# 32 unused bytes among the constants, which move the address of every tile allocated after them

## The chip, the cores and the metric

The kernel runs on one core of one Trainium2 chip. Its time is device microseconds of one execution. Three runs of the kernel before took 2201.70, 2201.96 and 2203.12 us; the median is 2201.96 us.

## What is computed

The reference runs sink-and-window attention on 4 batches of 8 heads, 768 tokens and head size 64, and feeds the result, as 3072 tokens of 512 features, to 8 experts whose weights come from a Sinkhorn iteration:

```
scores = scale * q @ k.T, kept where key < 4 or 0 <= query - key < 128
a = exp(scores - max) / (sum + 1e-9);   x = (a @ v) as 3072 x 512
P = exp(x @ w_gate - max); 8 times: P /= row sums; P /= column sums; P *= N / E
for e in range(8): out += P[:, e:e+1] * (max(x @ w1[e], 0) @ w2[e])     # 512 -> 1024 -> 512
```

## The kernel before

The whole of it is float32, and accuracy is kept by splitting an operand into a rounded half (type fp32r) and the rest; a product then has three matmuls (half by half, half by rest, rest by half).

**Attention, 0 to about 347 us.** Units of 128 queries and four heads; TensorE makes transposes (L428, L488, L504), scores (L467) and values (L524), and fills its gaps with the first expert's plain products for the first 1024 tokens (L598, with 256 columns, and L614, with 512).

**Part 0, about 347 to 942 us.** Experts 1 to 7 on the same 1024 tokens. An expert's hidden layer is cut into units of 256 columns, 28 in all. The first product of a unit (`first`, `product`, L725) is made as seven products of half size, named M1 to M7, on sums and differences of blocks: each is six matmuls of 128x128 by 128x512. The second product (`second`, L993) takes eight tiles of 128 tokens, each six matmuls with h, the hidden block, as the stationary operand and W2f, the weights, as the moving one. `STEPS` (L1030) lays them out: 15 steps of six matmuls, or 90 in a unit. The second product belongs to the unit before. h has one buffer in either of two pools, which take turns: `hps` (L1128) is `hp0` for even units and `hpr` for odd ones. Meanwhile the split weights are written to device memory for later (w1s, w2s), and SyncE's queue carries that traffic.

**Parts 1 and 2, about 942 to 2190 us.** All 8 experts on tokens 1024 to 3071, 1024 a part, 32 units a part. The first product is L725 again, 42 matmuls a unit, with W1q (reloaded split weights) stationary and the blocks B11, B21, B22 or T1 to T4 of x moving. The second product (`second2`, L1296) is seven products of half size as well, 42 matmuls a unit, with W2q stationary and hf, the split hidden layer, moving. `STEPS2` lays out one step of L725 and then one or two of L1296: three steps of L725 (M2, M1, M5) follow each other at a unit's start. A list by hand (`tick`, `at`) sets the order of all this; no scheduler moves it.

A matmul in the program is a pair of instructions: LDWEIGHTS reads the stationary operand, 128 columns, and MATMUL streams the moving one past it. The profile lists them as PEld and PE.

**Where tiles lie.** Each tile pool is a stretch of a partition's bytes. Pools that name no side are stacked from the bottom up, in the order in which they are opened: `const`, `xpool`, `accp`, and then the pools of each stage. Pools with `side="right"` are stacked from the top down: `hpr`, `w2pr`, `b12` (L360), `wa` and `rawp` of the attention stage, and later `w2q` and `accq` (L1395). In `const` the tiles of the Sinkhorn iteration are made after Xt.

Of the kernel before, what the change touches and what calls it, by code (L numbers as in the profile page):

```python
# [9 lines left out]
F32 = mybir.dt.float32  # L10
# [6 lines left out]
P = 128  # L17
# [212 lines left out]
def tile_sink_attention_moe(ctx: ExitStack, tc: tile.TileContext, q, k, v, wg, w1, w2, out):  # L230
# [27 lines left out]
    const = ctx.enter_context(tc.tile_pool(name="const", bufs=1))  # L258
# [56 lines left out]
        nc.vector.tensor_add(sel, ident[0:2 * E, 0:E], ident[0:2 * E, E:2 * E])  # L315

    Xt = const.tile([P, NT + 1, E + 1], F32, name="Xt")
    Pt = Xt[:, 0:NT, 0:E]

    xscr = dram.tile([KC, P, N], F32, name="xscr")  # L320
# [1128 lines left out]
```

## Time and profile before

| | us |
|---|---|
| median of three runs | 2201.96 |
| the profiled execution | 2202.73 |
| its span on the core | 2200.9 |
| TensorE busy (PE) | 2170.2, 99% of the span |
| TensorE weight loads (PEld), beside PE | 1774.1, 81% |
| VectorE (DVE) | 1561.5, 71% |
| ScalarE (ACT) | 893.1, 41% |
| GpSimd (POOL) | 742.5, 34% |
| DMA, share of 16 engines' time | 65.9% |

A busy PE is not PE at its peak: matmuls are pipelined, so what tells their price is how far their starts, or whole pieces of a chain, lie apart. The median is 0.77 us under the profiled execution.

### The profile page before, as it was taken

To read this page: it belongs to the slowest core of one execution; us is meant where nothing else is said; L and a number is where in the kernel's file an instruction comes from. 1 tells how busy PE (TensorE), PEld (TensorE's weight loads), DVE (VectorE), ACT (ScalarE), POOL (GpSimd) and SP (SyncE) were. 2 spreads that over 40 slices of the span, in tenths; PEclk is the share of its full clock that TensorE was granted. 3 is DMA by queue.
4 is the path that set the end of the run, shared out by engine and by line. 5 is a ranking of instruction groups with operands and counts; after the bars stand their busy time and mean duration, and the time that the engine had idled before them with its cause. 6 is when DMAs were issued, how large, how long until landed. Compare 5 with 4: busy or idle time off the path is not lost.

```text
span 2200.9 us, 31963 instructions
## 1 busy us (share of the span) xinstructions
PE 2170.2 (99%) x10525; PEld 1774.1 (81%) x10525; DVE 1561.5 (71%) x2888; ACT 893.1 (41%) x1914; POOL 742.5 (34%) x963
## 2 busy tenths in 40 slices
PE   7999999999999999999999999999999999999998
PEld 5888887788888888788888888888788888888886
DVE  8878868777777776776666666666756666666666
ACT  6777753544444443433323332322333233323222
POOL 6655544233233232133222233222332222332322
PEclk9999999999999999999999999999999999999999
DMA  6333324989898987776666666667866666666662
GB/s 169 87 81 89 81 88 151 313 285 308 280 313 278 315 275 240 247 268 202 191 198 200 197 190 200 203 191 244 301 198 198 201 200 192 199 202 188 201 192 82
DMA packets 395819, 453.31 MB, mean 206 GB/s; under 512 B 99648, under 2 KB 263680, under 8 KB 394752
## 3 DMA queue, kind: packets, MB, share of 16 engines
q1 hardware_dynamic: 395648, 451.20, 65.9%
q8 instruction: 86, 1.41, 0.3%
q14 instruction: 85, 0.70, 0.1%
HBM read 313.64 MB, written 137.46 MB: 205 GB/s over the span
## 4 chain that ended last, share of the span: by engine, by line
PE 92%; DVE 4%; ACT 2%; issue 1%; POOL 1%; DMA 0%; SPq 0%; DVEq 0%; ACTq 0%; POOLq 0%
PE c L725 39%; PE o L1296 20%; PE held L1296 8%; PE o L993 7%; PE held L993 7%; PE O L524 3%; PE ps L467 2%; PE g L598 2%; PE pt L488 2%; PE o L614 1%; PE pt L428 1%; ACT sc L473 1%; DVE T L752 0%; PE O L554 0%; DVE PT L351 0%
## 5 line engine op out<-in xcount | busy, mean ns | idle before, releaser
L751 ACT CAST hf<-w 128x512 fp32r<-128x512 f32 x448 | 265.7, 621 | 564.8 <-POOL w L1263 301.6
L1296 PE MATMUL o<-hf,W2q 128*128 128x512 f32 x1920 | 483.5, 395 | 0.0
L1296 PEld LDWEIGHTS o<-hf,W2q 128*128 128x128 f32 x1920 | 360.2, 188 | 85.7 <-DVE acc L1307 0.5
L725 PE MATMUL c<-T,W1q 128*128 128x512 f32 x1530 | 391.5, 391 | 0.0
L752 DVE TENSOR_TENSOR hf<-w,hf 128x512 fp32r<-128x512 f32 x448 | 330.4, 766 | 61.4 <-ACT hf L751 54.7
L1307 DVE TENSOR_TENSOR acc<-o,acc 128x512 f32<-128x512 f32 x300 | 206.6, 689 | 187.0 <-PE o L1296 186.8
L725 PEld LDWEIGHTS c<-T,W1q 128*128 128x128 f32 x1530 | 287.0, 188 | 63.3 <-ACT M L1240 0.4
L725 PE MATMUL c<-B,W1q 128*128 128x512 f32 x1134 | 279.3, 390 | 0.0
L1263 POOL TENSOR_TENSOR w<-w 128x512 f32<-128x512 f32 x64 | 83.2, 1300 | 513.2 <-DVE w L1245 508.0
L725 PEld LDWEIGHTS c<-B,W1q 128*128 128x128 f32 x1134 | 212.7, 188 | 46.2
L1244 DVE TENSOR_TENSOR w<-c,M 128x512 f32<-128x512 f32 x192 | 132.7, 691 | 153.1 <-PE c L725 148.3
L1240 ACT COPY M<-c 128x512 f32<-128x512 f32 x192 | 112.8, 588 | 264.8 <-PE c L725 264.0
L1296 PE MATMUL held<-hf,W2q 128*128 128x512 f32 x768 | 199.1, 395 | 0.0
L725 PE MATMUL c<-T,W1f 128*128 128x512 f32 x672 | 174.2, 394 | 2.0 <-DVE C L964 1.7
L993 PE MATMUL held<-W2f,h 128*128 128x512 f32 x672 | 173.7, 393 | 0.0
L993 PE MATMUL o<-W2f,h 128*128 128x512 f32 x672 | 173.7, 394 | 0.0
L1296 PEld LDWEIGHTS held<-hf,W2q 128*128 128x128 f32 x768 | 144.0, 188 | 33.5
L1278 POOL TENSOR_TENSOR w<-w 128x512 f32<-128x512 f32 x64 | 105.7, 1652 | 177.7 <-DVE hf L752 177.7
L814 POOL TENSOR_TENSOR r<-r 128x256 f32<-128x256 f32 x28 | 20.7, 740 | 397.1 <-ACT M L956 236.1
L725 PEld LDWEIGHTS c<-T,W1f 128*128 128x128 f32 x672 | 125.7, 188 | 32.4 <-issue 2.4
L993 PEld LDWEIGHTS o<-W2f,h 128*128 128x128 f32 x672 | 126.1, 188 | 29.6 <-DVE acc L1000 0.3
L993 PEld LDWEIGHTS held<-W2f,h 128*128 128x128 f32 x672 | 125.9, 188 | 29.0
(205 smaller groups left out, 3143.4 us busy)
## 6 DMA issues: line engine op xcount, KB each, us to landing
W2q<-w2s SPq DMA_DIRECT2D x448, 256.0 KB
W1q<-w1s SPq DMA_DIRECT2D x444, 256.0 KB
w1s<-W1f SPq DMA_DIRECT2D x56, 896.0 KB
w2s<-WT SPq DMA_DIRECT2D x136, 256.0 KB
r<-in_moe_w_dram SPq DMA_DIRECT2D x64, 512.0 KB
w2s<-W2f SPq DMA_DIRECT2D x56, 256.0 KB
PB<-psd SPq DMA_DIRECT2D x16, 512.0 KB
w2s<-W2f SPq DMA_DIRECT2D x56, 128.0 KB
```

What stands on the lines that cost most here:

```text
L467: nc.tensor.matmul(ps[h], lhsT=Q[r0:r0 + D, a, pr, :], rhs=K[r0:r0 + D, c, pr, :], start=(j == 0), stop=(j == 2))
L524: nc.tensor.matmul(u["O"][:, pr], lhsT=x_, rhs=y_, start=(j == 0), stop=(j == len(ops) - 1))
L725: nc.tensor.matmul(ps, lhsT=w1(a, k), rhs=x[:, b, k, :], start=(start and j == 0), stop=(stop and j == len(TERMS) - 1), skip_group_check=n ...
L751: nc.scalar.copy(dst[:, 0], src)
L752: at(1, lambda: nc.vector.tensor_sub(dst[:, 1], src, f32(dst[:, 0])))
L993: nc.tensor.matmul(o, lhsT=h[c, th][:, a, off:off + P], rhs=W2F[n][:, w, c, :], start=(begin and c == 0 and j == 0), stop=(end and c == 1 ...
L1240: nc.scalar.copy(t, T["c2"])
L1244: nc.vector.tensor_add(w, T["c1"], T[m])
L1263: nc.gpsimd.tensor_sub(S3, T["A11"], T["A21"])
L1278: at(k, lambda: nc.gpsimd.tensor_sub(T["A11"], w, T["A11"]))
L1296: nc.tensor.matmul(o, lhsT=W2Q[part, n, m][:, a, k * P:(k + 1) * P], rhs=F[part, n, H_OF[m]][:, w, :], start=(j == 0 and (begin or not hol ...
L1307: nc.vector.tensor_add(sums[m, k], o, sums[m, k])
```

## The change

```diff
     Xt = const.tile([P, NT + 1, E + 1], F32, name="Xt")
+
+    const.tile([P, 8], F32, name="pad")
     Pt = Xt[:, 0:NT, 0:E]
```

The new tile is 32 bytes in each partition. Nothing reads or writes it. All five engines have the same instructions in the same order as before, on the same tiles; no row of their order differs but for line numbers, which are two higher behind the new lines.

What differs are addresses. Everything that the left stack allocates after Xt lies 32 bytes higher; the right stack, ident, ones and Xt stay. In bytes within a partition, modulo 512 (all tiles of a row agree, since their sizes and the offsets within them are multiples of 512):

| tiles | used as | before | after |
|---|---|---|---|
| B11, B21, B22, T1 to T4 (left) | moving in L725 | 448 | 480 |
| W1f (left, part 0), W1q (left, parts 1 and 2) | stationary in L725 | 448 | 480 |
| h of pool hp0 (left; units 0, 2, ...) | stationary in L993 | 448 | 480 |
| h of pool hpr (right; units 1, 3, ...) | stationary in L993 | 480 | 480 |
| W2f (right) | moving in L993, L614 | 480 | 480 |
| hf (left) | moving in L1296 | 448 | 480 |
| W2q (right) | stationary in L1296 | 480 | 480 |
| W1 (right), B12 (right) | stationary, and one of four moving blocks, in L598 | 480 | 480 |
| PT and V (left) | both operands in L524 | 288 | 320 |
| ident (left, ahead of the new tile) | moving in the transposes | 288 | 288 |
| accumulators, copies, sums, raw weights of the experts (left) | other engines, DMA | 448 | 480 |

448 is a multiple of 64, and 480 is 32 more than one.

## Rows read from the trace of the kernel before

**Rows 1.** The page: the chain of waits, share of the span by engine and line.
```profile
PE 92%; DVE 4%; ACT 2%; issue 1%; POOL 1%; DMA 0%; SPq 0%; DVEq 0%; ACTq 0%; POOLq 0%
PE c L725 39%; PE o L1296 20%; PE held L1296 8%; PE o L993 7%; PE held L993 7%; PE O L524 3%; PE ps L467 2%; PE g L598 2%; PE pt L488 2%; PE o L614 1%; PE pt L428 1%; ACT sc L473 1%; DVE T L752 0%; PE O L554 0%; DVE PT L351 0%
```

**Rows 2.** Busy time by stretch: start:end, length, then by engine; clock, DMA share.
```profile
0.00:347.00 347.00, 329.15 (x2529) 279.76 (x2530) 275.14 (x976) 237.30 (x746) 207.44 (x495) 1.00 0.39 97
390.00:930.00 540.00, 539.46 (x2335) 437.51 (x2334) 400.13 (x606) 241.89 (x449) 155.26 (x191) 1.00 0.87 287
970.00:1570.00 600.00, 600.00 (x2605) 488.79 (x2604) 396.71 (x579) 182.63 (x316) 174.97 (x127) 1.00 0.69 215
1595.00:2170.00 575.00, 575.00 (x2497) 468.40 (x2497) 379.25 (x556) 177.65 (x307) 165.14 (x119) 1.00 0.64 193
```

**Rows 3.** Waits of PE, 390 to 2180 us: total us, times, longest.
```profile
PE c L725 <- DVE h L960: 1.8, 1, 1.8
...
PE c L725 <- ACT M L956: 0.2, 1, 0.2
```

**Rows 4.** The page: the granted clock in 40 slices of the span.
```profile
PEclk9999999999999999999999999999999999999999
```

**Rows 5.** Chain of waits, part 1, one unit: start us, us, what.
```profile
1312.59 4.09 PE c L725 x18
1316.68 1.39 PE held L1296 x6
1318.08 1.37 PE c L725 x6
1319.45 1.40 PE o L1296 x6
1320.84 1.37 PE c L725 x6
1322.22 2.79 PE o L1296 x12
...
1331.94 4.09 PE c L725 x18
```

**Rows 6.** Chain of waits, part 0, second product from hpr, then from hp0.
```profile
557.10 4.12 PE c L725 x18
561.22 1.38 PE o L993 x6
...
566.74 1.38 PE o L993 x6
568.13 1.37 PE held L993 x6
569.50 1.39 PE c L725 x6
...
577.79 4.11 PE c L725 x18
581.90 1.40 PE o L993 x6
...
587.47 1.40 PE o L993 x6
588.87 1.40 PE held L993 x6
...
598.66 4.12 PE c L725 x18
```

**Rows 7.** Chain of waits in attention, around three pieces of L598.
```profile
208.97 0.90 PE g L598 x6
...
211.25 0.70 PE o L614 x3
...
215.16 0.91 PE g L598 x6
...
221.76 0.90 PE g L598 x6
```

**Rows 8.** Line 960 on DVE in those units: durations ns min/median/max.
```profile
L960 DVE SCALAR_TENSOR_TENSOR h<-C,h x3: 691/693/693, 561.4 to 572.3; 128x512 fp32r<-128x512 f32 x3
L960 DVE SCALAR_TENSOR_TENSOR h<-C,h x3: 692/692/1225, 582.0 to 594.3; 128x512 fp32r<-128x512 f32 x3
```

**Rows 9.** Busy time in these two units of part 0, as in Rows 2.
```profile
557.10:577.79 20.69, 20.69 (x91) 16.89 (x91) 13.81 (x22) 9.04 (x17) 4.31 (x6) 1.00 0.97 309
577.79:598.66 20.87, 20.87 (x91) 16.90 (x91) 15.01 (x22) 9.31 (x17) 8.00 (x10) 1.00 0.76 241
```

## The prediction

> **What bounds the kernel now.** I read the chain of waits first: 92% of it is TensorE, and the lines L725, L1296 and L993 alone hold 39, 28 and 14% [rows 1]. The table of stretches then says where that is strict: from 390 to 930 us PE is busy 539.46 of 540 us, from 970 to 1570 and from 1595 to 2170 us all the time, while DVE, the next engine, has 400, 397 and 379 us of work there [rows 2]. The list of waits agrees: from 390 to 2180 us its longest entry is a single wait of 1.8 us [rows 3]. The clock is granted in full in every slice [rows 4], 1.00 in these stretches [rows 2], which is the level of 2.4 GHz. So in some 1750 us of the span the time is the number of matmuls times the distance of their starts, and nothing else. A change that moves no instruction can act there only through that distance.
>
> The distance is not one number. In part 1 a piece of six matmuls of L725 takes 1.37 us, a piece of six of L1296 1.39 to 1.40, though both stream 512 columns against 128x128 weights [rows 5]. Eighteen of L725 in a row take 4.09 us. The twelve by which that piece is longer than a piece of six took 4.09 - 1.37 = 2.72 us: 226.7 ns each, with no border in them. That is the price of a matmul whose neighbours are of its own kind: L725, both operands at 448. L1296 has moving hf at 448 and stationary W2q at 480, and pays 1.40 / 6 = 233 ns, 6.6 ns more.
>
> Two kinds of work could differ for another reason than addresses, so I looked for one line whose operand changes place. In part 0 the second product L993 streams W2f, at 480, in all units; h lies at 480 in one unit (pool hpr) and at 448 in the next (hp0). The pieces take 1.38 and, where a second one follows directly, 1.37 us in the first case, and 1.40 us each in the second [rows 6]. Length, shape, weights and order of the steps are the same. The units last 577.79 - 557.10 = 20.69 and 598.66 - 577.79 = 20.87 us. Four combinations of the two residues are thus in the trace: equal at 448, 226.7 ns; equal at 480, 228 ns in the piece that follows its own kind (its last matmul already borders on L725); unequal either way, 233 ns. The address that counts is that of one operand against the other, or else something that goes with it (rivals below). Borders cost as well: where the work passes from one residue to another a piece of L725 takes 1.37 to 1.39, not the 1.36 us of six times 226.7 ns [rows 5, 6].
>
> **The change part by part.** It adds no instruction, DMA or wait, and removes none. Its only effect is that the left stack lies 32 bytes higher, and then every matmul of L725, L993 and L1296 has both operands at 480, and every border is between equals.
>
> *Parts 1 and 2.* A unit lasts 1331.94 - 1312.59 = 19.35 us [rows 5] and has 42 + 42 = 84 matmuls. At 226.7 ns they take 19.04 us: 0.31 us less a unit, 19.8 us in 64 units. The stretches in which PE never stops give the same without a choice of unit: 600 - 2605 x 0.2267 = 9.5 and 575 - 2497 x 0.2267 = 8.9 us [rows 2], 18.4 together. They leave out about 50 us of the two parts, in which some matmuls wait for other things. I take 19.
>
> *Part 0.* A unit has 90 matmuls, 20.40 us at 226.7 ns. The unit with h at 480 gains 20.69 - 20.40 = 0.29, the one with h at 448 0.47 us [rows 6]; with 13 of each in the steady stretch that is 3.8 + 6.1 = 9.9 us. From the stretch: 540 - 2335 x 0.2267 = 10.7 [rows 2], of which 0.5 is idle time of PE. I take 10.
>
> *Attention.* All matmuls there but L614 have 264 columns or fewer. L598 streams B22 (448), B12 (480) and again B22 against weights at 480 in the three pieces shown, and takes 0.90, 0.91 and 0.90 us [rows 7]: at 256 columns the residue shows nothing. PE and the others take turns there (PE busy 329 of 347 us, DVE 275 [rows 2]). I count 0, and 2 us to either side for the range.
>
> *The other engines.* Their tiles go from a multiple of 64 to 32 past one. DVE's L960 writes h to hp0 (448) and to hpr (480) in turns: medians of 692 and 693 ns [rows 8]. I take no cost from this. What hides one if it is there: DVE is busy 400 of 540 us in part 0 and 66% later [rows 2]. *DMA.* No row separates packets by address. The cover is that the queue is no bound: its share is 0.87 in part 0 at most [rows 2], and in the fullest unit shown 0.97 of 20.69 = 20.07 us [rows 9], still below the 20.40 us that PE would need. So the shortening fits even there, but hardly: 1.6% more transfer time would use that room up, in such units. Bounds: 0, and for the 13 full units of part 0 their 0.29 us each, 3.8 us.
>
> The sum is 19 + 10 = 29 us. Against the profiled execution 2202.73 - 29 = 2173.7 us; the median of the runs lies 0.77 us lower, so 2173 us.
>
> **The rivals.**
> *The place counts, not the residue* (or the change does not do what it is meant to). In the trace before, operands with equal residues also lie in the same stack: B, T, W1q all left, W2f and h of hpr both right; unequal ones lie one left, one right. If the distance or the region makes the 6.6 ns, 32 bytes change nothing: 2202 us. For it: the two can't be told apart in parts 0 to 2, and in attention neither shows at 256 columns [rows 7]. Against it: the pieces of L725 that have both operands left pay more just beside a border [rows 5, 6], so what went before matters, which a mere region would not explain. The Trainium skill, TensorE: Matmul & The Clock Gate, "Step-by-step: what each phase is for", says that TensorE reads the streamed operand and the weights through two independent ports, and that loading the next weights takes no read bandwidth from the running matmul. By that rule no pairing of addresses should matter, and the sum would be 0; the 1.40 against 1.38 us of L993 disagrees [rows 6].
>
> *Half of it.* The mismatch inside pieces goes, the borders stay dear, since it is the change of line and not of residue that unsettles the stream. For it: L614's pieces of three, with equal residues, take 0.70 us, 233 ns each, among other work [rows 7]. Then a piece of L1296 falls from 1.40 to the 1.37 of L725: 14 pieces of six in a unit make 19.18 us, 0.17 less, 11 us in 64 units; in part 0 the odd units become like the even, 13 x 0.18 = 2 us. Together 13: 2189 us.
>
> *480 is bad in itself.* All pieces that touch 480 are slower than those that touch only 448, and the change takes everything there. If each then paid the 233.3 ns of today's mixed pieces, a unit of 84 would take 19.60 us, 0.25 more, 16 us in 64 units; one of 90 would take 21.0 against 20.78 on average, 0.22 more, 6 us in 26. That is 22 us slower, 2224 us. It decides once a pair at 480 costs more than about 230.4 ns (19.35 / 84) on average. Against it: the pair with both operands at 480 is the fastest that touches 480, 1.37 us in the second of two pieces [rows 6].
>
> **How the numbers follow.** Chances: the whole gain 0.70, half of it 0.16, no effect 0.10, slower 0.04. 0.2% is 4.4 us, about what a measurement of this kernel can tell from no change; the first two cases are faster by more. So faster 0.86, same 0.10, slower 0.04. The forecast is 2173. The range goes up to the half case, 2189, and down to 2167: 2 us of attention, and 4 us for borders that I count at their rounded prices.
>
> **What would show it.** Pieces of six of L1296 at 1.36 us and the piece of 18 at 4.08; units of 19.04 us in parts 1 and 2; in part 0 all units alike at 20.40, whichever pool holds h; DVE's L960 still at 692 ns; PE without waits from 390 to 2170 us, the granted clock at 1.00. Pieces of L1296 that stay at 1.40 mean that the place counts; 1.40 in L725 too, that 480 is bad; 1.37 to 1.39 with units of 19.2, that borders are dear in themselves. New waits of PE on DMA or of SyncE's queue in part 0 would mean that the transfers became the bound.

## The result, and the profile after

| | kernel before | changed kernel |
|---|---|---|
| median, us | 2202.54 (4 runs) | 2172.51 (4 runs, 2171.77 to 2173.66) |
| the profiled execution's span, us | 2200.9 | 2169.8 |

The ratio is 0.9864, 95% interval [0.9847, 0.9881]: 1.4% faster, 30.0 us. The forecast was 2173 us, with a range from 2167 to 2189.

The chain of waits of the page after, by engine and by line, answers to [rows 1]; the lines are numbered two higher, so L727, L995 and L1298 are the former L725, L993 and L1296. The granted clock over the span answers to [rows 4].

```profile
PEclk9999999999999999999999999999999999999999
...
PE 92%; DVE 4%; ACT 1%; issue 1%; POOL 1%; DMA 0%; SPq 0%; DVEq 0%; POOLq 0%; ACTq 0%
PE c L727 39%; PE o L1298 20%; PE held L1298 8%; PE held L995 7%; PE o L995 7%; PE O L526 3%; PE ps L469 2%; PE g L600 2%; PE pt L490 2%; PE o L616 1%; PE pt L430 1%; DVE T L754 0%; ACT sc L475 0%; PE O L556 0%; PE o L1357 0%
```

The engine that bounds the kernel, the shares of its lines and its clock are what they were. The time went where the pieces of that chain lie. In part 1 after (chain of waits: start us, us, what), answering to [rows 5]:

```profile
1276.31 4.08 PE c L727 x18
1280.39 1.36 PE o L1298 x6
1281.75 1.36 PE c L727 x6
1283.11 1.36 PE held L1298 x6
...
1285.83 2.72 PE o L1298 x12
...
1295.35 4.08 PE c L727 x18
```

Each piece of six takes 1.36 us, of whichever line, and the pieces of 12 and 18 are twice and three times that: on average there is one distance of starts, 226.7 ns, inside pieces and across borders (a border is a place in the chain where one line's piece ends and another's begins). A unit takes 1295.35 - 1276.31 = 19.04 us, where it took 19.35. The same view of part 0, answering to [rows 6]:

```profile
552.16 4.08 PE c L727 x18
556.24 1.36 PE o L995 x6
557.61 1.36 PE c L727 x6
...
561.68 1.36 PE o L995 x6
563.04 1.36 PE held L995 x6
...
572.57 4.08 PE c L727 x18
576.64 1.36 PE o L995 x6
...
583.45 1.36 PE held L995 x6
```

The two kinds of unit, with h in either pool, can no longer be told apart: the first lasts 572.57 - 552.16 = 20.41 us.

The table of stretches gives the whole stages: the two stretches of before (part 0, from its first matmul to the first with W1q; then parts 1 and 2, to the last with W2q), each stage with start:end, length, busy time by engine, clock and DMA share,

```profile
347.00:941.80 594.80, 590.37 (x2546) 476.82 (x2545) 447.78 (x690) 267.96 (x496) 171.44 (x206) 1.00 0.84 278
941.80:2190.40 1248.60, 1247.16 (x5428) 1014.89 (x5427) 835.82 (x1220) 385.56 (x668) 363.59 (x262) 1.00 0.65 202
```

the same two stretches after, and below them the two units of part 0, which answer to [rows 9]:

```profile
345.70:930.40 584.70, 579.18 (x2546) 475.35 (x2545) 446.99 (x690) 267.74 (x496) 172.18 (x206) 1.00 0.86 283
930.40:2159.30 1228.90, 1227.23 (x5429) 1014.74 (x5428) 832.21 (x1220) 385.16 (x668) 363.80 (x262) 1.00 0.66 205
...
552.16:572.57 20.41, 20.41 (x92) 16.90 (x91) 13.95 (x23) 9.04 (x17) 4.30 (x6) 1.00 1.00 316
572.57:592.96 20.39, 20.39 (x91) 16.88 (x91) 14.55 (x21) 9.30 (x17) 8.47 (x10) 1.00 0.80 253
```

Part 0 lost 594.8 - 584.7 = 10.1 us, parts 1 and 2 lost 1248.6 - 1228.9 = 19.7 us. Attention ends 1.3 us earlier, which two single profiles do not tell from nothing. The numbers of matmuls, and the busy times of the weight loads and of the other engines, hardly differ (DVE's fell by 4.4 us over both stretches). What fell is PE's own time, by 31.1 us.

### The profile page after: what moved, and what is told of

It is laid out like the page before. It is cut to its first block, busy times and chain, and to the rows that moved or that the text cites. A ratio compares the mean times of both kernels' runs of the same rounds, so it can differ in the third digit from the quotient of the medians.

```text
span 2169.8 us, 31963 instructions
## 1 busy us (share of the span) xinstructions
PE 2138.9 (99%) x10525; PEld 1772.4 (82%) x10525; DVE 1555.7 (72%) x2888; ACT 892.3 (41%) x1914; POOL 742.5 (34%) x963
## 4 chain that ended last, share of the span: by engine, by line
PE 92%; DVE 4%; ACT 1%; issue 1%; POOL 1%; DMA 0%; SPq 0%; DVEq 0%; POOLq 0%; ACTq 0%
PE c L727 39%; PE o L1298 20%; PE held L1298 8%; PE held L995 7%; PE o L995 7%; PE O L526 3%; PE ps L469 2%; PE g L600 2%; PE pt L490 2%; PE o L616 1%; PE pt L430 1%; DVE T L754 0%; ACT sc L475 0%; PE O L556 0%; PE o L1357 0%
## 5 line engine op out<-in xcount | busy, mean ns | idle before, releaser
L1298 PE MATMUL o<-hf,W2q 128*128 128x512 f32 x1920 | 471.9, 389 | 0.1
L1298 PEld LDWEIGHTS o<-hf,W2q 128*128 128x128 f32 x1920 | 360.2, 188 | 75.2 <-DVE acc L1309 0.6
L727 PE MATMUL c<-T,W1q 128*128 128x512 f32 x1530 | 388.7, 390 | 0.0
L727 PEld LDWEIGHTS c<-T,W1q 128*128 128x128 f32 x1530 | 286.9, 188 | 60.0 <-ACT M L1242 0.4
L727 PE MATMUL c<-B,W1q 128*128 128x512 f32 x1134 | 278.4, 390 | 0.0
L727 PEld LDWEIGHTS c<-B,W1q 128*128 128x128 f32 x1134 | 212.6, 188 | 44.1
L1298 PE MATMUL held<-hf,W2q 128*128 128x512 f32 x768 | 194.8, 390 | 0.0
L727 PE MATMUL c<-T,W1f 128*128 128x512 f32 x672 | 171.5, 390 | 2.3 <-DVE C L966 2.0
L995 PE MATMUL held<-W2f,h 128*128 128x512 f32 x672 | 171.0, 390 | 0.5 <-DVE W2f L754 0.5
L995 PE MATMUL o<-W2f,h 128*128 128x512 f32 x672 | 170.6, 390 | 0.2 <-DVE acc L1002 0.2
L1298 PEld LDWEIGHTS held<-hf,W2q 128*128 128x128 f32 x768 | 144.0, 188 | 29.8
L727 PEld LDWEIGHTS c<-T,W1f 128*128 128x128 f32 x672 | 125.7, 188 | 30.2 <-issue 2.4
L995 PEld LDWEIGHTS o<-W2f,h 128*128 128x128 f32 x672 | 125.9, 188 | 27.1 <-DVE acc L1002 1.0
L995 PEld LDWEIGHTS held<-W2f,h 128*128 128x128 f32 x672 | 125.9, 188 | 26.9 <-DVE W2f L754 0.9
```

Source lines behind the costliest of these rows:

```text
L727: nc.tensor.matmul(ps, lhsT=w1(a, k), rhs=x[:, b, k, :], start=(start and j == 0), stop=(stop and j == len(TERMS) - 1), skip_group_check=n ...
L995: nc.tensor.matmul(o, lhsT=h[c, th][:, a, off:off + P], rhs=W2F[n][:, w, c, :], start=(begin and c == 0 and j == 0), stop=(end and c == 1 ...
L1298: nc.tensor.matmul(o, lhsT=W2Q[part, n, m][:, a, k * P:(k + 1) * P], rhs=F[part, n, H_OF[m]][:, w, :], start=(j == 0 and (begin or not hol ...
```

## The experiments

After the result the theory was: what costs is that the moving and the stationary operand of a matmul lie at different residues, and that the moving stream passes from one residue to another at a border. The rivals were that the left stack's new place itself helped (480 being good, or the neighbourhood of tiles), and that the residue modulo 512, which the change aims at, is more than is needed. All seven kernels keep the order of the work and all its arithmetic; they differ in unused bytes alone.

**Everything at 448, by a pad on the other side.** The kernel before, with

```diff
+    right(ctx, "rpad", 1).tile([P, 8], F32, name="rpad")
     hpr, w2pr, b12p = right(p0r, "hpr", 1), right(p0r, "w2pr", 2), right(p0r, "b12", 1)
```

> The kernel before with 32 unused bytes at the top of the right stack instead of the left: every operand of L725, L993 and L1296 lies at 448, a multiple of 64. If only the one operand's residue against the other's counts: all pieces of six at 1.36 us, units of 19.04 and 20.40 us, ratio to the kernel before 0.986. If what helped was that the left operands came to 480: nothing is gained in L725 and L1296, whose moving operands stay at 448, ratio 0.995 to 1.00.

Measured: 2173.29 us, ratio to before 0.9867 [0.9851, 0.9883], the same as the change. Its chain of waits in part 1 (lines one higher than before):

```profile
1296.56 4.08 PE c L726 x18
1300.64 1.36 PE held L1297 x6
1302.00 1.36 PE c L726 x6
```

The left stack lies where it lay in the kernel before, and the whole gain is there. So it is not the place of the left operands, nor 480 as such: equality is what counts, of residues modulo 512 so far.

**A pad of 64 bytes.** Left operands at 0, right ones at 480.

```diff
-    const.tile([P, 8], F32, name="pad")
+    const.tile([P, 16], F32, name="pad")
```

> The new tile has 64 bytes, so the left stack lies at 0 modulo 512 and the right one at 480. If the relative residue counts: unequal again, pieces of L1296 at 1.40 us, units of part 1 at 19.35 us, ratio 1.00. If any shift of the left stack off its old place helps (another neighbourhood of tiles in memory): ratio 0.986.

Measured: 2203.84 us, ratio 1.0006 [0.9996, 1.0015]: no gain. Chain of waits in part 1:

```profile
1311.00 4.12 PE c L727 x18
1315.12 1.40 PE held L1298 x6
1316.52 1.38 PE c L727 x6
```

A shift as such does nothing, nor does it help that the left operands now begin at a multiple of 64 and of 512. L727 is even a shade dearer in this kernel than in the one before (1.38 and 4.12 against 1.37 and 4.09), though all moving operands of parts 1 and 2 now lie at 0 and only the stationary one changes from line to line.

**A pad of 96 bytes.** Left operands at 32, right ones at 480: equal modulo 64 only.

```diff
-    const.tile([P, 8], F32, name="pad")
+    const.tile([P, 24], F32, name="pad")
```

> The new tile has 96 bytes: left operands at 32 modulo 512, right ones at 480, so they agree modulo 64 and differ modulo 128, 256 and 512. If the residue modulo 64 is what counts: as with 32 bytes, pieces of L1296 at 1.36 us, ratio 0.986. If it must be the residue modulo 512, as the change says: as before, 1.40 us, ratio 1.00.

Measured: 2186.74 us, ratio 0.9930 [0.9913, 0.9946]. Neither expectation held: half of the gain came. Chain of waits, two pieces of part 0 in a unit with h in hp0, then part 1:

```profile
584.82 1.40 PE o L995 x6
586.22 1.40 PE held L995 x6
...
1305.26 4.08 PE c L727 x18
1309.34 1.37 PE held L1298 x6
1310.72 1.36 PE c L727 x6
1312.08 1.38 PE o L1298 x6
...
1314.81 2.75 PE o L1298 x12
```

L1298, whose moving operand lies 64 bytes past the stationary one, pays 1.37 to 1.38 us, and 2.75 for a piece of 12, where 2.72 is the matched price and 2.79 the old one: somewhat under half of its old surcharge. L727 pays nothing beside its borders here, 1.36 and 4.08. L995 with h in hp0, where the moving operand lies 64 bytes behind (480 against 32, counted round modulo 512), pays the full 1.40. Equality modulo 64 is not enough. At 64 bytes the sign of the difference seems to count, but the two signs stand in two different lines; at 32 bytes both signs paid 1.39 to 1.40 [rows 5, 6].

**Pads of 160 and 288 bytes.** Left operands at 96 (equal modulo 128) and at 224 (equal modulo 256).

```diff
-    const.tile([P, 8], F32, name="pad")
+    const.tile([P, 40], F32, name="pad")      # in the other kernel [P, 72]
```

> The new tile has 160 bytes: left operands at 96 modulo 512, right ones at 480, equal modulo 128, unequal modulo 256. With 96 bytes (equal modulo 64 alone) half of the gain came, 2186.7 us. If 128 is the period of what counts: pieces of L1296 at 1.36 us, ratio to before 0.986. If it is 512: pieces of L1296 between 1.37 and 1.40 us, ratio 0.990 to 1.00.

> The new tile has 288 bytes: left operands at 224 modulo 512, right ones at 480, equal modulo 256, unequal modulo 512. If the period is 256 or less: pieces of L1296 at 1.36 us, ratio 0.986. If only equality modulo 512 is without cost: pieces between 1.37 and 1.40 us, ratio 0.990 to 1.00.

Measured: with 160 bytes 2200.60 us, ratio 0.9988 [0.9979, 0.9998]; with 288 bytes 2173.76 us, ratio 0.9868 [0.9850, 0.9886]. Chain of waits in part 1 with 160 bytes,

```profile
1308.65 4.09 PE c L727 x18
1312.74 1.40 PE held L1298 x6
1314.14 1.37 PE c L727 x6
```

and with 288 bytes:

```profile
1297.66 4.08 PE c L727 x18
1301.74 1.36 PE held L1298 x6
1303.10 1.36 PE c L727 x6
```

Operands that differ by 256 bytes modulo 512 pay nothing; 128 bytes apart they pay in full. Among the differences tried, all of them multiples of 32, what has to agree is the address modulo 256. The table of residues modulo 512 asks for more than that.

**The moving operand of one line alone.** The changed kernel, with hf at 0 and W2q still at 480:

```diff
-        w1p, pb, cp, wp, hp = pool_("w1q", W1N), pool_("pb", 2), pool_("cq", 1), pool_("wq", 6), pool_("hq", 16)
+        w1p, pb, cp, wp = pool_("w1q", W1N), pool_("pb", 2), pool_("cq", 1), pool_("wq", 6)
+        pool_("hpad", 1).tile([P, 8], F32, name="hpad")
+        hp = pool_("hq", 16)
```

> The changed kernel with 32 more unused bytes ahead of the pool of hf alone: in L1296 the moving operand lies at 0 and the stationary one at 480, all else at 480. If the residue of one operand against the other counts: pieces of L1296 at 1.40 us, 2688 x 6.6 ns = 18 us more than the changed kernel, ratio to before 0.994. If besides a moving stream that passes to another residue at a border is dear for some matmuls, as in part 0 of the kernel before: pieces of six of L725 in parts 1 and 2 at 1.38 us instead of 1.36, up to 8 us more, ratio 0.998. Part 0 keeps its 20.40 us a unit in either case.

Measured: 2199.13 us, ratio 0.9985 [0.9976, 0.9995], 26.6 us more than the changed kernel: the second expectation. Chain of waits in part 1 (L1300 is L1298 of the changed kernel):

```profile
1303.52 4.11 PE c L727 x18
1307.62 1.40 PE held L1300 x6
1309.03 1.39 PE c L727 x6
1310.41 1.40 PE o L1300 x6
```

L727 has equal operands in this kernel, and its single pieces still take 1.39 us, more than the 1.37 of the kernel before. There it was the stationary operand that changed its residue from line to line, while all moving operands lay at 448; here it is the moving one. But that a border is dear only where the moving stream changes is not so: with the pad of 64 bytes only the stationary operand changes, and a piece of 18 of L727 takes 4.12 us, no less than the 4.11 here.

**The border alone.** The same, with hf and W2q both at 448 and the rest at 480, so that each matmul has equal operands:

```diff
+        pool_("hpad", 1).tile([P, 120], F32, name="hpad")     # ahead of the pool of hf
...
+            pool_("wpad", 1, side="right").tile([P, 8], F32, name="wpad")     # ahead of the pool of W2q
```

> The changed kernel with hf and W2q both moved, to 448 modulo 512, and all else at 480: in parts 1 and 2 each matmul has equal operands, but the residue changes at every border between L725 and L1296. If a border of two residues has a price of its own: the first piece after a border at 1.38 us, pieces that follow their own kind at 1.36; some 10 pieces a unit with 20 ns each, 64 units, 13 us more than the changed kernel, ratio to before 0.992. If only unequal operands within a pair cost: 1.36 us throughout, ratio 0.986. If lines are dear to each other for another reason than residues, the changed kernel would have shown it already, and it does not.

Measured: 2185.72 us, ratio 0.9924 [0.9906, 0.9942], 13.2 us more than the changed kernel, as the first expectation had it in its sum. Chain of waits in part 1:

```profile
1304.35 1.39 PE held L1300 x6
1305.74 1.38 PE c L727 x6
1307.12 1.38 PE o L1300 x6
1308.50 1.38 PE c L727 x6
1309.88 2.74 PE o L1300 x12
```

Pieces at a border pay 1.37 to 1.39 us, and the piece of 12 takes 2.74 for a matched 2.72. The starts in the trace show where the surcharge sits: in this piece of 12 they lie 230, 233 and 231 ns apart at first, then 226 to 227, and the last matmul lies 235 ns before the first of L727. So both ends of this piece pay, and its middle has the matched price. In part 0 of the kernel before, a first piece of L993 from hpr took 1.38 and a second one 1.37 [rows 6], which fits.

*What the two ends are.* While the last matmul of a piece streams, the weights of the next line are loaded already, as in part 1 of the kernel before at 1316.29 us (timeline: start us, us, engine, line):

```profile
1316.29 0.40 PE L725 MATMUL c<-T,W1q 128*128 128x512 f32 x1
1316.29 0.42 PEld L1296 LDWEIGHTS held<-hf,W2q 128*128 128x128 f32 x2
1316.52 0.39 PE L1296 MATMUL held<-hf,W2q 128*128 128x512 f32 x1
```

In the pieces of 18 from 1200 to 1500 us, the last matmul of the line of L725 takes 235 ns on average in the kernel before (stream at 448, next weights at 480), with the pad of 64 bytes (0 and 480) and in this kernel (480 and 448), though its own weights lie where its stream does. With hf alone moved, stream and next weights both lie at 480, and it takes 226.6. The next line's own pair does not decide it: that pair is unequal with hf alone moved, and equal in this kernel. All four kernels fit one reading: what counts is the running stream against the weights loaded during it. Inside a piece these weights have the residue of the piece's own, so the reading agrees with the theory there; at a border they are the next line's. In this kernel too, then, an unequal pair stands at each border. The start of a piece pays as well: in one piece of 18 each, the distances are down to 226 to 227 ns from the second start on in the kernel before, from the sixth with hf alone moved, from the eighth with the pad of 64 bytes and in this kernel. What sets that number stays open.

## Why the prediction was right

**The bound.** PE still never waits in the steady stretches. The list of waits of PE after, from 390 to 2150 us (total us, times, longest), has one longer entry, as [rows 3] had:

```profile
PE c L727 <- DVE h L962: 1.9, 1, 1.9
```

**The price of a matched matmul.** 226.7 ns was read as the difference of two pieces of L725. After the change it is the price in all of parts 0 to 2, 1.36 / 6. The reading was sound: in the trace before, all the starts in the middle of that piece of 18 lie 226 to 227 ns apart, and the two borders cancel in the difference.

**Parts 1 and 2, part 0.** 19 us were forecast and 19.7 came; 10 were forecast and 10.1 came. The prediction said that its stretches leave out about 50 us of parts 1 and 2; it is 1248.6 - 600 - 575 = 74 us, which at its own price of 18.4 us in 1175 add 1.2 us, or 19.6 in all. Units came to 19.04 and, in part 0, 20.41 and 20.39, for 19.04 and 20.40.

**Attention.** Counted at 0; it ended 1.3 us earlier in the one profile. Its pieces of the same lines after, answering to [rows 7], still take 0.91, 0.70 and 0.91 us (L600 and L616, formerly L598 and L614):

```profile
208.07 0.91 PE g L600 x6
210.35 0.70 PE o L616 x3
214.26 0.91 PE g L600 x6
```

L600 streams only 480 now, and gained nothing: with 256 columns among other work, no residue shows here. Why L616 still takes 233 ns for each of its three matmuls was not tried. Attention's own operands lie at yet other residues, so its pieces have borders on either side, and the experiment on borders fits that; this is argued and not shown.

**Other engines.** Nothing to pay. The line of DVE that writes h, once to the pool hpr and once to hp0, answers to [rows 8]:

```profile
L962 DVE SCALAR_TENSOR_TENSOR h<-C,h x3: 691/692/694, 556.4 to 567.2; 128x512 fp32r<-128x512 f32 x3
L962 DVE SCALAR_TENSOR_TENSOR h<-C,h x3: 691/693/1047, 576.8 to 588.9; 128x512 fp32r<-128x512 f32 x3
```

**DMA.** The fit in part 0 was as narrow as it was said to be: the share of the fuller unit went from 0.97 to 1.00. No wait of PE came of it in the steady stretch; the unit after it has room (0.80).

**The rivals.** *The place counts* fell with the result: hf and W2q still lie in different stacks, and pay 1.36. *480 is bad* fell with it, and the kernel with all at 448 shows that neither residue is better. *Half of it* named a real price, that of borders, but gave it to the change of line; in the changed kernel the lines change as often and no border costs. The price belongs to the change of residue, and the kernel with the border alone has it.

The Trainium skill, TensorE: Matmul & The Clock Gate, "Step-by-step: what each phase is for", says that weights and stream come through two ports of their own and that loading does not take read bandwidth from the running matmul. What the prediction drew from it, that no pairing of addresses should matter for the time, does not hold for these matmuls: with the same two reads in flight, 1.36 or 1.40 us a piece hang on how their addresses stand to each other. Whether it is read bandwidth that is lost, and where, no run here shows.

## What to carry to other kernels

Where TensorE never waits, compare pieces of equal shape in the chain of waits: 1.37 beside 1.40 us was the whole finding, and an operand that changes its buffer between otherwise equal steps is a free experiment. Give the stationary and the moving operands of long fp32r products the same address modulo 256 bytes, and all products that alternate the same one too; a pad of a few bytes ahead of one of two stacks is enough. Look again after each change in the constants, since any odd tile shifts one stack against the other.

## What was not expected

Moving minus stationary address, in the lines with 512 columns, and what a piece of six and a piece of 12 took, over all kernels (the single pieces stand beside borders; L993 and L995 have no piece of 12 in one line of the view, so two pieces in a row are added):

| difference, bytes modulo 512 | seen in | six, us | twelve, us |
|---|---|---|---|
| 0 | changed kernel; all at 448 | 1.36 | 2.72 |
| 256 | pad of 288, L1298 | 1.36 | 2.72 |
| 64 | pad of 96, L1298 | 1.37 to 1.38 | 2.75 |
| 448 (64 behind) | pad of 96, L995 from hp0 | 1.40 | 2.80 |
| 32 and 480 (32 behind) | kernel before, L993 from hp0 and L1296; pad of 64, L1298 | 1.39 to 1.40 | 2.79 to 2.80 |
| 128 | pad of 160, L1298 | 1.40 | 2.80 |

That 64 bytes ahead cost under half, 64 behind all, and 128 all again was not foreseen. Nor was it that borders cost at both ends of a piece: 1.37 to 1.39 us for six matmuls that are all matched among themselves.
